# Key and value loads of a decode attention kernel issued from two engines instead of one

## The chip, the cores and the metric

The kernel runs on one core of a Trainium2 chip. The metric is device time in microseconds (us), from launch to end; it ran three times before the change, and a profiled execution of the same kernel gives the trace.

In the profile PE is TensorE (matmuls), PEld its weight loads, DVE is VectorE, ACT is ScalarE, POOL is GpSimd and SP is SyncE. A name with a q at its end (SPq, ACTq, PEq) is the sequencer of that engine, which issues DMAs and waits on semaphores. A DMA queue is shown by a number: q1 is the queue of SP's loads, q10 the queue of ACT's. All queues are worked off by the same 16 DMA engines of the core.

## The reference

One decode step of a transformer block for two tokens (one of each batch row), all in fp32. The attention part reads a cache of keys and values for 32 heads, 8192 positions and 128 channels:

```python
q = (x @ wq)                                    # per head, after a layer norm of x
scores = einsum("bhqd,bhkd->bhqk", q, k_cache) * (Dh ** -0.5)
o = einsum("bhqk,bhkd->bhqd", softmax(scores), v_cache)
h = x + o.reshape(B, 1, H * Dh) @ wo
h2 = h + squared_relu(layernorm(h) @ w1 + b1) @ w2 + b2
```

With B = 2, H = 32 there are 64 pairs (head, batch row), and each pair's keys and values are 2 x 8192 x 128 fp32 values, 8 MB. These 64 loads are 537 of the 561 MB that the kernel reads.

## The kernel before

**The ring.** SBUF holds three slots of 64 KB a partition (`ring[0]` to `ring[2]`, one tensor `slots`). One load, `kvd[i]`, brings all keys and values of pair `i` into slot `i % 3` in one DMA of 128 rows of 64 KB. The projection weights `wq` come first, into slot 2; pairs 0 and 1 go into slots 0 and 1. Every later load goes where an earlier pair has been worked off: load 2 into the slot of `wq`, load `i + 3` into the slot of pair `i`. When pairs 61 and 62 are done, their slots take the weights of the end: `wo` (two DMAs) goes into slot 1, `w1` and `w2` (one DMA and four) into slot 2. The last pair, 63, lies in slot 0.

**Who issues.** SP issues all these loads, each behind a wait for one token of the semaphore FREE (`p.take(sp, FREE)`, which waits for 1 and takes 1 away; line 97 holds the wait). DVE gives one token when the query vectors are ready (line 264) and one behind the last instruction of each pair (line 319). So load 2 takes the first token, load `i + 3` the token of pair `i`, `wo` that of pair 61 and `w1` that of pair 62. Each slot has a semaphore of its own, `LD[t]`, which a load raises by 16 when it has landed.

**A pair.** PE waits for the query column (QUERY) and for the slot's load, and forms the scores of the 8192 positions in two chunks of 4096 (`front`, 16 matmuls a chunk, into one PSUM tile `s[c]` of 128 x 1024 each); it needs the tile back from DVE (BUFFER). DVE takes each chunk's maximum (`maxes`), ACT the exponential with its sum (`exps`), and DVE multiplies the values in the slot by the weights and sums them: four products of 128 x 1024 a chunk (`product`). BUFFER is given behind each chunk's products, FREE behind both chunks. ACT does nothing else in this stage: its loop (line 304) is one pair long, and POOL is idle after it has built the identity at the start (lines 191 to 194).

**The end.** Once pair 62 is done, `shift(0, NG)` brings the pairs 0 to 61 to a common maximum (DVE, one matmul, ACT), then PE forms the scores of pair 63 (lines 405 to 411). The products of pair 63, the combination of all pairs, the projection by `wo`, the second layer norm and the two matmuls of the feed-forward part follow in one chain; PE waits for `w1` at line 467 and for each piece of `w2` at line 491. The result leaves in one small DMA.

Instructions of PE and DVE are recorded first and emitted later, so the profile gives them the one line of that helper, L54; SP's loads all have L159. The pairs' order is set by the program's loops and the semaphores alone; there is no planner.

Of the kernel before, what the change touches and what calls it, by code (L numbers as in the profile page):

```python
# [13 lines left out]
NC = 2  # L14
# [6 lines left out]
LAST = BH - 1  # L21
ROUNDS = LAST // 3
# [77 lines left out]
def attention_block_kernel(nc, xd, kvd, wqd, wod, w1d, w2d, out):  # L100
    p = Program(nc)
    pe, dve, act, pool, sp = p.pe, p.dve, nc.scalar, nc.gpsimd, nc.sync
# [5 lines left out]
    ring = [slots[:, k * ROW : (k + 1) * ROW] for k in range(3)]  # L108
# [42 lines left out]
    LD = [p.sem(f"load{k}") for k in range(3)]  # L151
    SM, LO = p.sem("small"), p.sem("wo_b")
    LW1 = p.sem("w1")
    LW2 = [p.sem(f"w2_{k}") for k in range(len(W2_PIECES))]
    FREE, SCORES, MAXED, EXPED, BUFFER, QUERY = (p.sem(n) for n in ("free", "scores", "maxed", "exped", "buffer", "query"))
    OUT = nc.alloc_semaphore("out")

    def load(tile, src, sem):
        sp.dma_start(tile, src).then_inc(sem, 16)  # L159
# [7 lines left out]
    load(ring[2], wqd, LD[2])  # L167
    load(ring[0], kvd[0], LD[0])
    load(ring[1], kvd[1], LD[1])
    with sp.Fori(0, ROUNDS - 1) as r:  # L170
        i = r * 3
        for u in range(3):
            t = (2 + u) % 3
            p.take(sp, FREE)
            load(ring[t], kvd[i + (2 + u)], LD[t])
    p.take(sp, FREE)
    load(ring[2], kvd[LAST - 1], LD[2])
    p.take(sp, FREE)
    load(ring[0], kvd[LAST], LD[0])
    p.take(sp, FREE)  # L180
    load(WO[:, :HA], wod[:, :HA], LD[1])
    load(WO[:, HA:], wod[:, HA:], LO)
    p.take(sp, FREE)
    load(ring[2][:, :W1_ROW], w1d, LW1)
    at = 0
    for k, n in enumerate(W2_PIECES):
# [5 lines left out]
    p.after("pool", t_id)  # L192
    t_id = p.tell("pool", pool.affine_select(out=ident, in_=ident, compare_op=ALU.not_equal, fill=1.0, base=0,
                                             pattern=[[-1, P]], channel_multiplier=1))
    dve.memset(ones_d, 1.0 / D)
    dve.memset(eps_t, EPS)
    dve.memset(zero, 0.0)
# [69 lines left out]
    def at(tile, pair, n, off=0, size=None):  # L267
        size = n if size is None else size
        return tile[:, bass.ds(pair * n + off, size)]
# [16 lines left out]
    def exps(pair, c):  # L286
        p.take(act, MAXED)
        act.activation(s[c], s[c], AF.Exp, bias=at(nm, pair, NC, c, 1), scale=1.0,  # L288
                       accum_out=at(ls, pair, NC, c, 1)).then_inc(EXPED, 1)
# [6 lines left out]
    first = pe.cut()  # L296
# [4 lines left out]
            front(c, ring[u])  # L301
    pairs = pe.cut()

    with act.Fori(0, ROUNDS * 3) as i:
        for c in range(NC):
            exps(i, c)

# [234 lines left out]
```

## Time and profile before

| | us |
|---|---|
| three runs, median (lowest to highest) | 1302.75 (1302.64 to 1302.89) |
| the profiled execution: its time | 1302.71 |
| its span, from the first to the last instruction | 1301.3 |
| DVE busy | 761.7 (59%) |
| PE busy | 401.4 (31%) |
| ACT busy | 160.3 (12%) |
| POOL busy | 0.7 (0%) |
| DMA: all bytes, mean rate | 561.13 MB, 431 GB/s |

The page gives busy times by engine, shares of the 16 DMA engines by queue, the chain of work that ended last, groups of instructions, and the DMA issues with the time from issue to landing. A timeline gives instructions in order of time; behind a row stands in brackets how long its engine had been idle before it and who ended that. A row that merges several instructions shows their count behind an x, and the stretch from the first to the last. A view by windows gives, for any stretch, the busy time of each engine, the DMA engines' share and rate. Packets are counted in it by their start, so a window of a few us is coarse: one packet of 64 KB counts whole or not at all.

### The profile page before, as it was taken

The numbers are of one execution on the slowest core, as the hardware profiler recorded it, in microseconds if no ns is written. First come the engines' busy times: TensorE is split into PE (matmuls) and PEld (weight loads), VectorE is DVE, ScalarE is ACT, GpSimd is POOL, SyncE is SP. The second block draws the span as 40 slices with busy tenths as digits, with TensorE's granted clock in tenths as the row PEclk, the third lists the DMA queues.
The fourth block names the chain that finished last, engine by engine and source line by source line (L and its number), as shares of the span: only waits on it lengthen the run. The fifth ranks groups of instructions, "written<-read, shape, count | busy, mean of one in ns | idle before, by whom it ended". The sixth has DMA issues, their size and how long they took to land. (4 is left out here: it accounts for less than half of the span.)

```text
span 1301.3 us, 8752 instructions
## 1 busy us (share of the span) xinstructions
PE 401.4 (31%) x2384; PEld 107.9 (8%) x2384; DVE 761.7 (59%) x1267; ACT 160.3 (12%) x268; POOL 0.7 (0%) x6
## 2 busy tenths in 40 slices
PE   3223223323323313313313322322322331331347
PEld 1000000000000000000000000000000000000013
DVE  1375565575565566566466566557457556556564
ACT  0011011011011011111111101101101101101111
POOL 0000000000000000000000000000000000000000
PEclk9576666566666667666666657666666756666668
DMA  9999999999999999999999999999999999999998
GB/s 419 419 449 421 448 421 449 421 437 433 423 445 423 447 423 447 421 443 427 429 439 423 447 423 447 421 447 423 437 433 423 445 423 447 423 447 421 439 423 368
DMA packets 10520, 561.13 MB, mean 431 GB/s; under 512 B 1170, under 2 KB 1298, under 8 KB 1556
## 3 DMA queue, kind: packets, MB, share of 16 engines
q1 hardware_dynamic: 10512, 561.07, 99.7%
q8 instruction: 3, 0.05, 0.0%
q14 instruction: 1, 0.01, 0.0%
q10 hardware_dynamic: 4, 0.00, 0.0%
HBM read 561.00 MB, written 0.07 MB: 431 GB/s over the span
## 5 line engine op out<-in xcount | busy, mean ns | idle before, releaser
L54 PE MATMUL s<-slots,qc 128*32 128x512 f32 x2048 | 362.6, 872 | 859.4 <-PEq L54 859.4
L54 DVE SCALAR_TENSOR_TENSOR slots<-slots,s 128x1024 f32 (+1 forms) x512 | 589.5, 1217 | 2.3 <-DVEq L54 1.0
L54 DVE TENSOR_REDUCE nm<-s 128x1024 f32 (+1 forms) x128 | 156.8, 1225 | 488.9 <-DVEq L54 488.9
L288 ACT ACTIVATE s<-s,nm 128x1024 f32<-128x1024 f32 x128 | 139.3, 1088 | 1090.9 <-ACTq L97 1090.9
L54 PEld LDWEIGHTS s<-slots,qc 128*32 128x32 f32 x2048 | 91.4, 153 | 1129.5 <-issue 1129.4
L54 DVE DVE_READ_ACCUMULATOR slots<-slots,s (+1 forms) x512 | 42.3, 83 | 0.0
L288 ACT ACTIVATION_READ_ACCUMULATOR s<-s,nm (+1 forms) x128 | 24.7, 193 | 0.0
L54 PE MATMUL s<-slots,xr 128*32 128x512 f32 (+1 forms) x96 | 12.6, 684 | 8.8 <-PEq L54 8.2
L54 DVE COPY qc<-qs 128x32 f32 (+1 forms) x64 | 11.0, 172 | 0.0
L54 DVE STREAM_TRANSPOSE big<-s 128x512 f32<-128x512 f32 x2 | 1.4, 718 | 16.1 <-PE s L54 16.1
L54 PE MATMUL pm<-slots,big 128*32 128x512 f32 x64 | 10.6, 782 | 0.0
L54 PE MATMUL pm<-nq,pick_all 128*128 128x496 f32 (+1 forms) x4 | 2.6, 742 | 17.3 <-DVE nq L54 17.3
L54 DVE COPY xT<-pm 128x8 f32<-128x8 f32 x1 | 0.2, 167 | 9.5 <-PE pm L54 9.5
L54 PE MATMUL pm<-ident,xrow 2*128 2x2 f32 x8 | 1.9, 350 | 10.4 <-DMA xrow<-in_x 10.4
L54 PEld LDWEIGHTS s<-slots,xr 128*32 128x32 f32 x96 | 3.5, 126 | 17.1 <-issue 15.7
L54 PE MATMUL s<-big,pick_all 128*128 128x512 f32 x8 | 4.5, 639 | 0.0
L54 PE MATMUL s<-slots,a 128*2 128x128 f32 x112 | 3.5, 272 | 0.9 <-DMA slots<-in_w2d 0.9
L54 PEld LDWEIGHTS pm<-slots,big 128*32 128x32 f32 x64 | 2.6, 138 | 5.6 <-issue 5.1
L54 PEld LDWEIGHTS s<-slots,a 128*2 128x2 f32 x112 | 2.7, 84 | 2.3 <-DVE a L54 1.5
L54 DVE COPY res<-s 128x128 f32<-128x128 f32 x1 | 0.3, 291 | 4.4 <-PE s L54 4.4
L54 PEld LDWEIGHTS pm<-ident,xrow 2*128 2x128 f32 x8 | 1.8, 322 | 10.4 <-DMA xrow<-in_x 10.4
L54 DVE TENSOR_REDUCE gm<-pm 128x62 f32<-128x496 f32 (+1 forms) x2 | 0.9, 426 | 2.9 <-PE pm L54 2.9
(64 smaller groups left out, 29.4 us busy)
## 6 DMA issues: line engine op xcount, KB each, us to landing
slots<-in_wod SPq DMA_DIRECT2D x1, 5120.0 KB, 33.6
slots<-in_w1d SPq DMA_DIRECT2D x1, 3593.0 KB, 31.1
slots<-in_wod SPq DMA_DIRECT2D x1, 3072.0 KB, 40.6
slots<-in_w2d SPq DMA_DIRECT2D x1, 2048.0 KB, 35.6
slots<-in_kvd SPq DMA_DIRECT2D x64, 41.1
slots<-in_w2d SPq DMA_DIRECT2D x1, 1024.0 KB, 37.6
slots<-in_w2d SPq DMA_DIRECT2D x2, 256.0 KB, 37.7
out<-res SPq DMA_DIRECT2D x1, 64.0 KB, 1.6
```

The lines of the kernel that those rows point to most:

```text
L54: ins = getattr(self.engine, op.name)(*op.args, **op.kwargs)
L288: act.activation(s[c], s[c], AF.Exp, bias=at(nm, pair, NC, c, 1), scale=1.0, accum_out=at(ls, pair, NC, c, 1)).then_inc(EXPED, 1)
```

## The change

Three things are written anew.

- SP keeps `wq`, the loads of pairs 0, 1 and 2, every later even pair (4, 6, up to 62), pair 63 and the weights of the end. It takes its tokens from a new semaphore FREE_SP.
- ACT issues the odd pairs 3, 5, up to 61 on its own queue, with tokens of another new semaphore FREE_ACT. For that its loop is unrolled over six pairs (ten rounds; the last three pairs have a small loop). Within each two pairs the load stands behind both exponentials of the even pair: ACT waits there until that even pair is done, then issues the load into its slot.
- POOL, behind the building of the identity, takes each token of FREE and hands it on by turns, the first to SP, then one to ACT and one to SP thirty times, then three to SP.

What DVE and PE do is unchanged, and so is which slot a load fills and which token it stands behind.

```diff
@@ semaphores
-    FREE, SCORES, MAXED, EXPED, BUFFER, QUERY = (p.sem(n) for n in ("free", "scores", "maxed", "exped", "buffer", "query"))
+    FREE, SCORES, MAXED, EXPED, BUFFER, QUERY, FREE_SP, FREE_ACT = (
+        p.sem(n) for n in ("free", "scores", "maxed", "exped", "buffer", "query", "free_sp", "free_act"))
@@ SP's loads
-    with sp.Fori(0, ROUNDS - 1) as r:
-        i = r * 3
+    with sp.Fori(0, (LAST - 3) // 6) as r:
         for u in range(3):
-            t = (2 + u) % 3
-            p.take(sp, FREE)
-            load(ring[t], kvd[i + (2 + u)], LD[t])
-    p.take(sp, FREE)
+            t = (2 + 2 * u) % 3
+            p.take(sp, FREE_SP)
+            load(ring[t], kvd[r * 6 + (2 + 2 * u)], LD[t])
+    p.take(sp, FREE_SP)
     load(ring[2], kvd[LAST - 1], LD[2])
-    p.take(sp, FREE)
+    p.take(sp, FREE_SP)
     load(ring[0], kvd[LAST], LD[0])
-    p.take(sp, FREE)
+    p.take(sp, FREE_SP)
     load(WO[:, :HA], wod[:, :HA], LD[1])
     load(WO[:, HA:], wod[:, HA:], LO)
-    p.take(sp, FREE)
+    p.take(sp, FREE_SP)
     load(ring[2][:, :W1_ROW], w1d, LW1)
@@ POOL, behind the identity
+    def hand_on(to):
+        p.take(pool, FREE)
+        pool.sem_inc(to, 1)
+
+    hand_on(FREE_SP)
+    with pool.Fori(0, (LAST - 3) // 2):
+        hand_on(FREE_ACT)
+        hand_on(FREE_SP)
+    with pool.Fori(0, 3):
+        hand_on(FREE_SP)
@@ ACT's loop
-    with act.Fori(0, ROUNDS * 3) as i:
+    def load_odd(first, t):
+        p.take(act, FREE_ACT)
+        act.dma_start(ring[t], kvd[first + 3]).then_inc(LD[t], 16)
+
+    with act.Fori(0, (LAST - 3) // 6) as r:
+        for u in range(3):
+            for k in range(2):
+                for c in range(NC):
+                    exps(r * 6 + (2 * u + k), c)
+                if k == 0:
+                    load_odd(r * 6 + 2 * u, (2 * u) % 3)
+    with act.Fori(LAST - 3, LAST) as i:
         for c in range(NC):
             exps(i, c)
```

ACT's loop over the pairs, as it stood (ISA is the wait for a maximum; in brackets the semaphore that a row waits for):

```order
L304 UNCONDITIONAL_BRANCH
L288 ISA [waits maxed]
L288 ACTIVATE s,ls<-s,nm 128x1024
L288 ISA [waits maxed]
L288 ACTIVATE s,ls<-s,nm 128x1024
L304 REGISTER_ALU
L304 COMPARE_AND_BRANCH
```

ACT's loop now, the first two of its six pairs:

```order
L319 UNCONDITIONAL_BRANCH
L299 ISA [waits maxed]
L299 ACTIVATE s,ls<-s,nm 128x1024
L299 ISA [waits maxed]
L299 ACTIVATE s,ls<-s,nm 128x1024
L317 ISA [waits free_act]
L317 DMA slots<-in_kvd 128x16384
L299 ISA [waits maxed]
L299 ACTIVATE s,ls<-s,nm 128x1024
L299 ISA [waits maxed]
L299 ACTIVATE s,ls<-s,nm 128x1024
```

Between the second exponential of an even pair and the first of the odd one ACT now waits for the slot's token and issues a load; the other four pairs of a round repeat these rows.

SP's program now, from the last of its loop's three loads to the weights of the end:

```order
L160 ISA [waits free_sp]
L160 DMA slots<-in_kvd 128x16384
L171 REGISTER_ALU
L171 COMPARE_AND_BRANCH
L160 DMA slots<-in_kvd 128x16384 [waits free_sp] x2
L160 DMA slots<-in_wod 128x10240 [waits free_sp]
L160 DMA slots<-in_wod 128x6144
L160 DMA slots<-in_w1d 128x7186 [waits free_sp]
L160 DMA slots<-in_w2d 128x4096
```

The rows read as they did but for the semaphore and the number of rounds, ten in place of twenty; loads 62 and 63 and all weights behind them stay on SP's queue, while load 61, the one ahead of 62, has gone to ACT's.

## The prediction

> **What bounds the kernel now.** I read the page's DMA queues first, then the windows over the pairs, then the chain and the timeline. The queues and the issues:
>
> ```profile
> q1 hardware_dynamic: 10512, 561.07, 99.7%
> slots<-in_kvd SPq DMA_DIRECT2D x64, 41.1
> ```
>
> SP's queue q1 alone keeps the 16 DMA engines busy for 99.7% of the span. The windows ask whether this holds in every stage. Their columns are the stretch and its length, then busy time (and count) of PE, PEld, DVE, ACT and POOL, the granted clock, the DMA engines' share and GB/s:
>
> ```profile
> 62.30:120.40 58.10, 16.51 (x96) 4.21 (x97) 35.08 (x57) 7.22 (x12) 0.00 (x0) 0.65 1.00 433
> 120.40:700.90 580.50, 171.06 (x960) 43.17 (x960) 350.83 (x570) 72.28 (x120) 0.00 (x0) 0.65 1.00 434
> 1165.80:1262.60 96.80, 29.87 (x162) 7.58 (x163) 59.41 (x97) 12.04 (x20) 0.00 (x0) 0.64 1.00 433
> ```
>
> The share is 1.00 and the rate 433 to 434 GB/s at the start, in the middle and at the end of the pairs, while DVE works 350.83 of 580.50 us. So the bytes bound the pairs, with no hole to fill. The timeline shows the beat: PE's first matmul of pairs 60 to 63, the SP issues behind the tokens of pairs 61 and 62, and DVE's rows of pair 62:
>
> ```profile
> 1204.57 5.57 PE L54 MATMUL s<-slots,qc 128*32 128x512 f32 x32 [14.34 <-PEq L54]
> 1223.91 6.13 PE L54 MATMUL s<-slots,qc 128*32 128x512 f32 x32 [13.78 <-PEq L54]
> 1240.89 0.80 SPq L159 DMA_DIRECT2D slots<-in_wod  x2
> 1243.26 5.00 PE L54 MATMUL s<-slots,qc 128*32 128x512 f32 x32 [13.22 <-PEq L54]
> 1246.91 1.22 DVE L54 TENSOR_REDUCE nm<-s 128x1024 f32 x1 [6.15 <-DVEq L54]
> 1248.53 1.23 DVE L54 TENSOR_REDUCE nm<-s 128x1024 f32 x1 [0.40 <-DVEq L54]
> 1259.26 0.33 SPq L159 DMA_DIRECT2D slots<-in_w1d  x1
> 1262.61 3.64 PE L54 MATMUL s<-slots,qc 128*32 128x512 f32 x16 [0.28 <-PEq L54]
> ```
>
> A load lands every 19.35 us (1223.91 to 1243.26). Pair 61 holds its slot for 1240.89 - 1223.91 = 17.0 us, pair 62 for 1259.26 - 1243.26 = 16.0; I take C = 16.5. When a token comes, the next load still lacks 19.35 - 16.5 = 2.85 us and the one after it is whole: 22.2 us of work are queued ahead of the new load, and 22.2 + 19.35 = 41.5 agrees with the 41.1 from issue to landing above. The end hangs on the last bytes:
>
> ```profile
> 1260.11 37.56 DMA slots<-in_w2d
> 1297.72 1.65 PE s L54 x48
> 1299.39 0.29 DVE res L54
> ```
>
> The chain is one DMA wait to 1297.7 and then 2 us of work. Only three things can move the time: the rate of the DMA engines, a hole in their work, or a compute chain of the end that comes later than the last weights.
>
> **The change part by part.** *Issuing.* ACT's issue and POOL's hop are new on the way from a token to a load.
>
> ```profile
> L224 ACTq DMA_DIRECT2D xrow<-in_x x1: 542/542/542, 2.8 to 2.8; - x1
> L159 SPq DMA_DIRECT2D slots<-in_kvd x64: 332/333/426, 1.2 to 1221.0; - x64
> 1.17 0.29 POOL L193 TENSOR_SCALAR_AFFINE_SELECT ident<-ident 128x128 f32<-128x128 f32 x1 [0.23 <-POOL ident L191]
> ```
>
> POOL's only measured wait on a semaphore cost 0.23 us; ACT issues in 0.54 us, SP in 0.33. So a load starts 0.23 to some 0.5 us later than before, and the queued work of many us hides it: 0. Behind ACT's new wait stand the exponentials of the odd pair. They need a maximum that DVE begins after the same token and that takes 1.22 us; ACT needs 0.23 + 0.54 = 0.8. So nothing is late there; without that cover it would be DVE's time, of which 580.50 - 350.83 = 230 of 580 us are idle: 0. The 30 issues that SP loses (30 x 0.33 us) were hidden already: 0. The Trainium skill (DMA: Bandwidth & Descriptors, section Issuing engines are not separate DMA queues) says that all issuers run on the same 16 DMA engines and that issuing from several saves only sequencer time; by it the sum has no term for the rate, and the row of 0.33 us, hidden, agrees.
>
> *Order of service.* Now two queues have loads at once. The trace has one such place: at 2.79 us ACT issues `xrow` (4 KB) on q10, behind three loads of SP. The two issues and PE's first use of `xrow` are from the timeline; the packets and queues are those of the window 2.7 to 10.4 us, from that issue to the landing:
>
> ```profile
> 0.75 0.39 SPq L159 DMA_DIRECT2D slots<-in_wqd  x1
> 2.79 0.54 ACTq L224 DMA_DIRECT2D xrow<-in_x  x1
> DMA packets 52, 3.15 MB, mean 409 GB/s; under 512 B 2, under 2 KB 2, under 8 KB 4
> q1 hardware_dynamic: 48, 3.15, 94.2%
> q10 hardware_dynamic: 4, 0.00, 0.2%
> 10.37 1.86 PE L54 MATMUL pm<-ident,xrow 2*128 2x2 f32 x8 [10.37 <-DMA xrow<-in_x]
> ```
>
> In 7.7 us q1 got 48 packets, three on each engine, and q10 was served in between; SP's three loads would have lasted 58 us. So the queues take turns by packets of about 2.4 us (a load is eight on each engine), and I take equal turns. What that does is worked out by hand. At the token that issues load i+3 let load i+1, ahead of it in its queue, lack r us, and load i+2 in the other queue s us. Both run at half rate, so i+1 lands after 2r. In the C that follow, the other two get C/2 = 8.25 each. At the next token the new s is 19.35 - 8.25 = 11.1 and the new r is s - r - 8.25 = 2.85 - r. So r swings between 0 and 2.85, and at least 11.1 us stay queued in place of 22.2. The engines never run dry, two pairs still take 2 x 16.5 + 2 x 2.85 = 38.7 us, and pairs 0 to 63 cost nothing more: 0.
>
> *The end.* Here the order counts. Load 61 is alone on ACT's queue; 60, 62, 63 and the weights are on SP's. When 62 is issued, 61 lacks 11.1 us and shares the engines until it lands, so 62 has by then got s - r = 8.25 to 11.1 us, in whole packets three or four of 2.4 us: pair 61 starts 7.3 to 11.1 us later than at 1223.91, and I take four packets, 9.7 us, 1233.6. Its token comes at 1233.6 + 16.5 = 1250.1, against 1240.89. Load 62 lands by 1243.26 as before, since all bytes through it have moved by then. So pair 62 follows pair 61 without a wait: its DVE rows take 1259.26 - 1246.91 = 12.35 us, and about 0.5 more, since the second chunk's tile comes back only with pair 61's end and its 16 matmuls then take 1.92 us:
>
> ```profile
> 1266.70 1.92 PE L54 MATMUL s<-slots,qc 128*32 128x512 f32 x16
> ```
>
> The 0.5 is 1.92 - 1.22 (the first maximum) - 0.40 (idle already in the 12.35) = 0.3, and 0.2 for the wait, by POOL's 0.23. That is 12.85. Its token comes at 1262.95, 3.7 us later; with 7.3 and 16.0, or 11.1 and 17.0, it would be 0.8 or 5.6. The DMA queue still holds load 63's rest and `wo` then, and 63 and the weights land when they did. What is late is the combination of the pairs that starts at this token, and with it the chain up to `w1`. That chain has the following slack:
>
> ```profile
> 1290.40 3.21 PE L54 MATMUL s<-slots,xr 128*32 128x448 f32 x32 [0.63 <-DMA slots<-in_w1d]
> 1295.33 1.93 PE L54 MATMUL s<-slots,a 128*2 128x128 f32 x64 [0.66 <-DMA slots<-in_w2d]
> 1297.72 1.60 PE L54 MATMUL s<-slots,a 128*2 128x128 f32 x48 [0.24 <-DMA slots<-in_w2d]
> ```
>
> With the 0.28 us before pair 63's scores (1262.61) PE waits 0.28 + 0.63 + 0.66 + 0.24 = 1.8 us for DMAs; part of the 0.66 is another wait, so I take 1.7. The end moves by 3.7 - 1.7 = +2.0 us, bounds 0 (0.8 is absorbed) and 5.6 - 1.7 = +3.9.
>
> *Sum.* 0 for the pairs, +2.0 at the end. The profiled execution's 1302.71 (0.04 under the median, span 1301.3) gives 1302.71 + 2.0 = **1304.7 us**, 1302.7 to 1306.6 by its own bounds. That is +0.15%. I count a difference up to 0.2%, 2.6 us, as the same: about what a measurement can tell.
>
> **The rivals.** *Order unchanged*: ACT's loads are served whole, as from one queue. Then landings keep their even beat, pair 62 ends on time, and the time is 1302.7. For it: descriptors may be made well ahead of the engines. Against it: `xrow`, served long before SP's queue was empty. The change would then not do what it says.
>
> *Two queues lose at each hand-over* (slower). Place: each packet from load 3 to load 63, 61 x 8 = 488 packets on an engine. It decides from 2.6 us / 488 = 5.3 ns a packet alone, from 1.2 ns together with the +2.0. Bounds: 0, and the 409 GB/s of the `xrow` window against 434, 6% of 61 x 19.35 us = 68 us, though that window counts whole packets (three of 2.4 us in 7.7 us are 94%), so it is nearer 0. I price it at twice the point, 5.2 us: 1302.7 + 2.0 + 5.2 = 1309.9.
>
> *Two queues gain at each hand-over* (faster): the next packet of one queue is prepared while the other's moves. [...] Against it: a share of 1.00 in every window. The windows resolve 1 GB/s of 434, 0.23% or 3 us, so up to 3 us can't be excluded: 1299.7, and if the end is late too, 1301.7. The Trainium skill (DMA: Bandwidth & Descriptors, section Where 436 GB/s comes from) puts the ceiling of the 16 ports at 435.2 GB/s; by it, as an estimate from that page, the rate could rise at most from 433.5 (8.389 MB in 19.35 us) by 0.4%, or about 5 us, to 1298; the 433 to 434 of the windows agree that little is left.
>
> **How the numbers follow.** Equal turns and a late end 0.60, of which 0.42 stay within 0.2% (a shift under 2.6 us lies in the lower two thirds of 0 to 3.9) and 0.18 lie above; order unchanged 0.12, the same; loss at hand-overs 0.14, slower; gain 0.11, faster; 0.03 for what I don't see, split between slower (0.02) and the same (0.01). Faster 0.11, the same 0.55, slower 0.34. The range holds the likeliest case and the unchanged order (0.72), and reaches down to 1300.0 and up to 1308.0 into the two rate cases until some 0.2 are left out.
>
> **What would show it.** In the changed profile the share in the windows stays 1.00 and the rate 433 to 434; a change of 1 GB/s or more there is one of the rate rivals. About half the bytes stand under q10 (30 loads, 252 MB). PE's first matmul of pair 61 comes near 1233.6 in place of 1223.9, and landings come in uneven steps between 16.5 and 22.2 us; an even 19.35 with pair 61 at 1223.9 means unchanged order. The `w1` issue moves from 1259.26 to about 1263, load 63's first matmul goes with it, and PE's waits for `w1` and `w2` shrink or vanish. The prediction is wrong if a window in the pairs falls under 1.00, or if ACT's wait for a maximum gives way to DVE waiting on ACT.

## The result

The changed kernel takes 1306.53 us (median of 8 runs, 1305.46 to 1308.54) against 1302.78 (8 runs, 1302.55 to 1302.89): a ratio of 1.003, 95% interval 1.0019 to 1.0041. It is slower, by about 3.8 us. The runs of the kernel before lie within 0.4 us, those of the changed one within 3.1.

The profiled execution is one of the fastest of the changed kernel, 1305.48 us with a span of 1303.9; a second profile of the same kernel (called *again* below) has 1307.57 and 1306.2. The queues of the changed kernel:

```profile
q1 hardware_dynamic: 6192, 309.41, 54.9%
q10 hardware_dynamic: 4324, 251.66, 44.6%
```

ACT's queue carries 30 loads, 252 MB, and the two together keep the engines as busy as one did (99.5% against 99.7%). Whether the rate suffers is seen from the bytes that have moved by a given time. The next rows are the windows 0 to 117, 0 to 300 and 0 to 1200 us, first of the kernel before:

```profile
DMA packets 852, 50.28 MB, mean 430 GB/s; under 512 B 82, under 2 KB 82, under 8 KB 84
DMA packets 2220, 129.40 MB, mean 431 GB/s; under 512 B 242, under 2 KB 242, under 8 KB 244
DMA packets 8914, 519.86 MB, mean 433 GB/s; under 512 B 978, under 2 KB 978, under 8 KB 980
```

and of the changed kernel:

```profile
DMA packets 852, 50.23 MB, mean 429 GB/s; under 512 B 82, under 2 KB 82, under 8 KB 84
DMA packets 2196, 128.82 MB, mean 429 GB/s; under 512 B 226, under 2 KB 226, under 8 KB 228
DMA packets 8902, 519.02 MB, mean 433 GB/s; under 512 B 978, under 2 KB 978, under 8 KB 980
```

At 433.5 MB a millisecond the changed kernel is 0.1 us behind at 117 us, 1.3 behind at 300 and 1.9 at 1200 (0.84 MB). These windows count packets by their start, so each is good to some 0.5 us. The trace's records of single packets say it more finely: between 118.7 and 120 us up to 14 of the 16 engines stand idle, nowhere else are more than one or two; the lag is 0.3 us before that and 1.9 to 2.1 from 250 us on, and it doesn't grow any more. So there is one hole, near 119 us, and no loss of rate in the thousand microseconds after it. The engines' idle time makes about half of it: the 16 engines lose 0.9 us of their time from 118 to 122 us. The rest lies in the first packets of the next load: ACT issues load 5 at 118.67, its packets start from 119.64 on, 1.0 us later, and each engine's first one takes 2.7 to 3.6 us in place of 2.42. The windows from 262 to 1262 us, the kernel before and the changed one, have the same rate:

```profile
262.00:1262.00 1000.00, 290.59 (x1634) 73.53 (x1634) 607.46 (x988) 124.96 (x208) 0.00 (x0) 0.65 1.00 433
262.00:1262.00 1000.00, 293.36 (x1664) 73.75 (x1664) 608.15 (x989) 125.36 (x208) 0.00 (x0) 0.65 1.00 433
```

The other part is the end. The changed kernel's first matmuls of pairs 61 and 62 and its later steps, from the timelines of PE and SP:

```profile
1234.62 6.08 PE L54 MATMUL s<-slots,qc 128*32 128x512 f32 x32 [13.83 <-PEq L54]
1246.99 3.30 PE L54 MATMUL s<-slots,qc 128*32 128x512 f32 x16 [6.29 <-PEq L54]
1251.56 1.92 PE L54 MATMUL s<-slots,qc 128*32 128x512 f32 x16 [1.26 <-PEq L54]
1251.68 0.80 SPq L160 DMA_DIRECT2D slots<-in_wod  x2
1264.75 0.33 SPq L160 DMA_DIRECT2D slots<-in_w1d  x1
1293.86 3.21 PE L54 MATMUL s<-slots,xr 128*32 128x448 f32 x32
1298.51 1.93 PE L54 MATMUL s<-slots,a 128*2 128x128 f32 x64 [0.38 <-DVE a L54]
```

Pair 61 starts 10.7 us later than before (1234.62 against 1223.91), the token of pair 62, which `w1` follows, comes 5.5 us later (1264.75 against 1259.26), and PE no longer waits for any weight: the bracket before `w1`'s matmuls is gone, and the one before `w2`'s names DVE. So the chain that ended last, which was one DMA wait before, now runs through the compute of the end (four of its 31 pieces; dots stand for the others):

```profile
1273.74 0.16 DVE slots L54
...
1278.70 7.34 PE pm L54 x42
...
1292.97 4.15 PE s L54 x34
...
1298.51 3.50 PE s L54 x120
```

### The profile page after: what moved, and what is told of

Its sections match the earlier page's. It is cut to its first block, busy times and chain, and to the rows that moved or that the text cites. A ratio compares the mean times of both kernels' runs of the same rounds, so it can differ in the third digit from the quotient of the medians.

```text
span 1303.9 us, 8771 instructions
## 1 busy us (share of the span) xinstructions
PE 403.5 (31%) x2384; PEld 107.2 (8%) x2384; DVE 761.4 (58%) x1267; ACT 160.4 (12%) x268; POOL 0.7 (0%) x6
## 5 line engine op out<-in xcount | busy, mean ns | idle before, releaser
L54 DVE TENSOR_REDUCE nm<-s 128x1024 f32 (+1 forms) x128 | 156.7, 1224 | 492.8 <-DVEq L54 492.8
L54 PEld LDWEIGHTS s<-slots,xr 128*32 128x32 f32 x96 | 3.5, 126 | 16.5 <-issue 16.5
```

The source lines that it names most:

```text
L54: ins = getattr(self.engine, op.name)(*op.args, **op.kwargs)
```

## The experiments

**Theory**: two queues take turns by packets. Where sharing begins, two loads land together and the next one stands in the queues alone, so the engines that finish it first may run dry: a hole, once. At the end load 61, alone on ACT's queue, is late by half a load, and the chain behind pair 62 with it. **Rivals**: each hand-over between the queues costs (3.8 us for 30 loads, 0.13 us a load); issuing through POOL and ACT costs; a second queue's first load has a fixed cost.

### One load on ACT's queue, in the middle

Based on the changed kernel; SP issues all loads but 33, and POOL hands 31 tokens to SP, one to ACT, 32 to SP.

```diff
-    with act.Fori(0, (LAST - 3) // 6) as r:
...
+    with act.Fori(0, 30) as i:
+        for c in range(NC):
+            exps(i, c)
+    for c in range(NC):
+        exps(30, c)
+    load_odd(30, 30 % 3)
+    with act.Fori(31, LAST) as i:
+        for c in range(NC):
+            exps(i, c)
```

> One load alone, 33, goes to ACT's queue; all others stay on SP's. Theory (a hole where sharing begins, and a late end): 32 and 33 land together, so for the 17 us of pair 32 only load 34 is queued, and the engines that finish it first stand idle, once, for about 1.4 us, near 700 us, as at 119 us in the changed kernel. Later the order is that of one queue and the end is on time behind the last byte: 1302.7 + 1.4 to 1.9 = 1304.1 to 1304.6. Rival (each hand-over between the queues costs): the changed kernel's +3.8 us for 30 loads is 0.13 us a load, so 1302.8 to 1302.9. Rival (issuing through POOL and ACT costs, by token): POOL hands on all 64 tokens here too, so 1305 to 1306.5.

Measured: 1304.80 us (11 runs, 1303.15 to 1305.63), a ratio of 1.0015 (1.0006 to 1.0023). One load of 64 on the second queue costs 1.9 us against its own series of the kernel before (1302.93), half of what 30 cost and 15 times the 0.13 us a load of the hand-over rival. The profile of this run was its fastest, so the kernel was run once more for another:

> Load 33 alone on ACT's queue once more, for a second profile: the first was the fastest of its eleven runs (1303.15 of up to 1305.63) and had almost no hole. Theory: a run near 1304.8 has its token of pair 32 later against the end of load 34, and bytes late by 1.5 to 2 us from 700 us on.

That run took 1304.63. Its matmuls of the pairs 31 to 33 (PE), then ACT's issue of load 33 and SP's of load 35:

```profile
643.67 5.56 PE L54 MATMUL s<-slots,qc 128*32 128x512 f32 x32 [14.36 <-PEq L54]
682.37 4.99 PE L54 MATMUL s<-slots,qc 128*32 128x512 f32 x32 [33.13 <-PEq L54]
693.80 3.64 PE L54 MATMUL s<-slots,qc 128*32 128x512 f32 x16 [6.45 <-PEq L54]
640.38 0.37 ACTq L323 DMA_DIRECT2D slots<-in_kvd  x1
698.65 0.34 SPq L160 DMA_DIRECT2D slots<-in_kvd  x1
```

and the bytes moved by 690 and by 1200 us:

```profile
DMA packets 5124, 298.74 MB, mean 433 GB/s; under 512 B 562, under 2 KB 562, under 8 KB 564
DMA packets 8902, 519.08 MB, mean 433 GB/s; under 512 B 978, under 2 KB 978, under 8 KB 980
```

Load 32 is a whole load late (682.37 - 643.67 = 38.7 us), pair 33 follows directly, and load 35 is issued at 698.65, when load 34 has been alone for some 16 us (by the events of its semaphore, load 33 had all landed at 682.9). The first of the 16 engines ended load 34 at 699.4, by the events of its semaphore. At 690 us the bytes are those of the kernel before to the packet; at 1200 they are 0.78 MB, 1.8 us, behind. The end is on time behind the bytes again. The hole is where the theory puts it; the expected 1304.1 to 1304.6 was just missed. In the fastest run load 32 came earlier by one packet's turn (first matmul at 679.85), load 35 was issued at 696.91, 2.6 us ahead of the first engine's end, and the bytes were 0.6 us behind at 1200 (by the single packets 0.3, against 1.5 in the other run).

### One load on ACT's queue, near the end

```diff
-    with act.Fori(0, (LAST - 3) // 6) as r:
...
+    with act.Fori(0, 58) as i:
+        for c in range(NC):
+            exps(i, c)
+    for c in range(NC):
+        exps(58, c)
+    load_odd(58, 58 % 3)
+    with act.Fori(59, LAST) as i:
+        for c in range(NC):
+            exps(i, c)
```

> One load alone, 61, goes to ACT's queue. Theory: 60 and 61 land together near 1224, pair 60 starts there in place of 1204.6, its token comes near 1241, 61 and 62 follow without a wait, 13 us each, so w1 is issued near 1267.3 in place of 1259.3; a hole of about 1.4 us falls at 1241. The chain from there to the end took 37.3 us in the changed kernel, so the end comes at 1304.6 in the span and the time is 1307.5 to 1308.5: more than with 30 loads on ACT's queue. Rival (each hand-over costs, 0.13 us a load): 1302.9. Rival (issuing through POOL costs): 1305 to 1306.5.

Measured: 1309.52 us (6 runs, 1305.62 to 1310.74), 1.0047 (1.0035 to 1.0059). The timeline of its profile (1309.11):

```profile
1224.00 5.02 PE L54 MATMUL s<-slots,qc 128*32 128x512 f32 x32 [33.11 <-PEq L54]
1235.46 3.64 PE L54 MATMUL s<-slots,qc 128*32 128x512 f32 x16 [6.45 <-PEq L54]
1249.96 3.64 PE L54 MATMUL s<-slots,qc 128*32 128x512 f32 x16 [6.28 <-PEq L54]
1240.15 0.33 SPq L160 DMA_DIRECT2D slots<-in_kvd  x1
1267.72 0.33 SPq L160 DMA_DIRECT2D slots<-in_w1d  x1
```

Pair 60 at 1224.0, its token at 1240.2, `w1` at 1267.7: as worked out (1224, 1241, 1267.3). The median came 1 us above the range; in the profile `w1` is 0.4 us later than worked out, and the chain from there took 41.4 us with what lies around the span, against 40.7 in the first profile of the changed kernel. The hole at 1241 is there too, somewhat smaller than expected: down to 6 of the 16 engines are busy, and 0.9 us are lost by the single packets. One load costs 6.6 us here, more than the 30 loads of the change, which neither a price by load nor one by hand-over can give.

### The last odd loads back on SP's queue

The changed kernel with 57, 59 and 61 on SP; POOL's alternation and ACT's six-pair loop end six pairs earlier.

```diff
-    with sp.Fori(0, (LAST - 3) // 6) as r:
+    with sp.Fori(0, 9) as r:
...
+    for i in range(56, LAST - 1):
+        p.take(sp, FREE_SP)
+        load(ring[i % 3], kvd[i], LD[i % 3])
```

> As the changed kernel, but the last three odd loads, 57, 59 and 61, stay on SP's queue. Theory: the hole at 119 us stays (bytes late by 1.9 us from there on), but the pairs of the end catch up, w1 is issued about 1.9 us later than before the change and no more, and the time is 1302.7 + 1.9 = 1304.6 (1304.2 to 1305.0), with less spread from run to run than the changed kernel's 1305.5 to 1308.5. Rival (each hand-over costs): 27 of 30 loads, 1306.1.

Measured: 1304.56 us (11 runs, 1303.32 to 1305.70), 1.0012 (1.0004 to 1.0021), at the expected 1304.6; the spread is 2.4 us against 3.1, little less. In its profile (1304.98) PE's waits for the weights are back, and the chain that ended last is again one DMA wait:

```profile
1262.01 0.33 SPq L160 DMA_DIRECT2D slots<-in_w1d  x1
1292.49 3.21 PE L54 MATMUL s<-slots,xr 128*32 128x448 f32 x32 [0.86 <-DMA slots<-in_w1d]
1297.42 1.93 PE L54 MATMUL s<-slots,a 128*2 128x128 f32 x64 [0.66 <-DMA slots<-in_w2d]
1299.80 1.61 PE L54 MATMUL s<-slots,a 128*2 128x128 f32 x48 [0.24 <-DMA slots<-in_w2d]
```

The piece of that chain, and the bytes moved by 1200 us:

```profile
1262.87 36.89 DMA slots<-in_w2d
DMA packets 8901, 518.95 MB, mean 432 GB/s; under 512 B 978, under 2 KB 978, under 8 KB 980
```

The bytes are 0.91 MB behind (518.95 against 519.86), 2.1 us, and the time is 2.3 above the kernel before's profile. So without the late end only the hole is left, and all of it is in the time.

### ACT's queue from load 33 on

```diff
+    with act.Fori(0, 30) as i:
+        for c in range(NC):
+            exps(i, c)
-    with act.Fori(0, (LAST - 3) // 6) as r:
+    with act.Fori(5, 10) as r:
```

> ACT issues only the odd loads 33 to 61, the first half stays on one queue. Theory: the hole of 1.4 to 1.9 us moves from 119 us to about 700 us, the end is as late as in the changed kernel, and the time is that of the changed kernel, 1305.5 to 1307, median near 1306.3. Rival (each hand-over costs): half the loads, 1304.6. Rival (the hole belongs to the start, by code loading or the like): no hole, 1304.5.

Measured: 1305.54 us (11 runs, 1303.96 to 1306.47), 1.0019 (1.0010 to 1.0028). This is at the lower edge of the expected range and above the rivals' 1304.5 and 1304.6, but by only 1 us in a spread of 2.5; the time alone would not tell them apart. The profile does, and it misses a part of the expectation. There is no hole at all, though one of 1.4 to 1.9 us was expected near 700 us (519.81 MB by 1200 us, 0.05 behind), and its 1306.24 comes from the end alone:

```profile
1233.83 5.52 PE L54 MATMUL s<-slots,qc 128*32 128x512 f32 x32 [14.40 <-PEq L54]
1250.21 3.64 PE L54 MATMUL s<-slots,qc 128*32 128x512 f32 x16 [0.93 <-PEq L54]
1264.83 0.33 SPq L160 DMA_DIRECT2D slots<-in_w1d  x1
1294.84 3.21 PE L54 MATMUL s<-slots,xr 128*32 128x448 f32 x32
```

ACT's issue of load 35, and the bytes moved by 1200 us:

```profile
697.05 0.34 ACTq L323 DMA_DIRECT2D slots<-in_kvd  x1
DMA packets 8914, 519.81 MB, mean 433 GB/s; under 512 B 978, under 2 KB 978, under 8 KB 980
```

No hole was also the sign of the rival that ties the hole to the start of the kernel. But load 33 alone had one at 699 us, so that rival is out. The issue of load 35 (697.05) says why there is none here: it comes 2.4 us ahead of the first engine's end of load 34 (699.49 by its semaphore), as in the fastest run of load 33 alone, where 2.6 us left almost no hole. A fixed cost of the second queue's first load would have shown here as well.

With the bytes on time, pair 61 is 9.9 us late (1233.83 against 1223.91) and `w1` 5.6. Together with the run before, where the bytes were late and the end was not, this separates the two parts of the cost.

### Issuing alone

First, all loads on SP, with POOL handing on each token; then all loads from 3 on, and the weights, on ACT's queue.

```diff
-    with pool.Fori(0, (LAST - 3) // 2):
-        hand_on(FREE_ACT)
-        hand_on(FREE_SP)
-    with pool.Fori(0, 3):
+    with pool.Fori(0, 64):
         hand_on(FREE_SP)
```

> All loads stay on SP's queue, but POOL hands every token on to SP. Theory (only the sharing of two queues costs): the later issue is hidden by 22 us of queued work, 1302.8, within 0.3 us of the kernel before. Rival (issuing through POOL costs, by token): 1305 to 1306.5.

```diff
+    with act.Fori(0, 20) as r:
+        for u in range(3):
+            for c in range(NC):
+                exps(r * 3 + u, c)
+            load_odd(r * 3 + u, u)
```

> ACT issues every load from 3 on, with the weights of the end, on its own queue; SP issues only wq and the loads 0 to 2. Theory: one queue at a time serves the loads in order, but there is one crossing at the start, where load 3 on ACT's queue shares with load 2: 2 and 3 land together near 102 us, then load 4 comes behind 3 on one queue; whether a hole opens at 119 us as in the changed kernel is the same question of one lone load, so up to 2 us there, nothing at the end: 1302.8 to 1304.8. Rival (ACT's issue or POOL's hop costs by load): twice the 30 loads' +3.8 us, 1310. Rival (hand-overs cost): 1302.9.

Measured: 1302.74 us with POOL's hop (11 runs, 1302.60 to 1303.12), 0.9999 (0.9990 to 1.0008): it costs nothing. With all on ACT 1304.20 (11 runs, 1303.39 to 1305.90), 1.0012 (1.0003 to 1.0021): with twice the issues of the change, less than half its loss, and the bytes of its profile are 0.85 MB, 2.0 us, behind by 1200 us (1.5 us by the single packets), with a hole again near 119 us. The profiled time, 1305.57, is 2.9 us longer than the kernel before's, more than the bytes say, because the hole does not make the 16 engines late alike: the last of them ends load 5 3.1 us later than before (142.60 against 139.48) and load 63 2.8 us later (1265.11 against 1262.32). What is left there is the one crossing from SP's queue to ACT's.

### A longer hold, to size the cover

Three DVE instructions that do nothing for the result, then seven, ahead of each pair's token, in the kernel before and in the one with load 33 alone.

```diff
             ins.then_inc(BUFFER, 1)
+        for extra, n in ((big, 8), (aw, 4), (acc, 4)):
+            row = pick_all[:, None, :].to_broadcast([P, n, P])
+            dve.tensor_tensor(extra.rearrange("p (a m) -> p a m", m=P), row, row, op=ALU.mult)
         dve.drain().then_inc(FREE, 1)
```

> The kernel before, with three idle DVE instructions (128 x 1024, 512 and 512) ahead of each pair's token, about 1.25 + 0.67 + 0.67 = 2.6 us a pair. Theory: a pair holds its slot 19.1 instead of 16.5 us, and the 22 us of queued work hide it in all pairs; the token of pair 62 comes 2.6 us later, of which the end's slack takes 1.7 or more: 1302.8 to 1303.7.

> The same three idle DVE instructions in the kernel with load 33 alone on ACT's queue. Theory: at the one place where load 34 is queued alone, there is no cover, so the later token lengthens the hole one to one: that kernel's +1.9 us grows to about 4.5 us over the kernel before with the same instructions, 1307 to 1308. Rival (each hand-over costs): the difference stays 0.1 us. Rival (a fixed cost of a second queue's first load): the difference stays 1.9 us.

> The kernel before with seven idle DVE instructions ahead of each pair's token, about 5.3 us a pair (with the three earlier ones of 2.4 us the token of pair 62 came 2.1 us later and the end absorbed all of it). Theory: the queued work still hides it in all pairs; the token of pair 62 comes about 5 us later, of which the end absorbs about 2.9: 1304.9 (1304 to 1306).

> The same seven instructions with load 33 alone on ACT's queue. Theory (no cover where load 34 is queued alone): a hole opens when the token of pair 32 comes less than about 2 us ahead of the first engine's end of load 34; in the two profiles so far it came 2.6 us ahead (bytes late by 0.25 us) and 0.9 us ahead (late by 1.25). Now it comes about 2 us behind, so the bytes are late by about 4 us from there on, and the time is that of the kernel before with the same instructions plus 3 to 5: 1309 (1308 to 1310). Rival (a fixed cost of the second queue's load): plus 1.9, 1306.8. Rival (each hand-over): plus 0.1, 1305.0.

| | kernel before | load 33 on ACT's queue |
|---|---|---|
| as it is | 1302.85 (33 runs) | 1304.80 (11 runs) |
| three more instructions | 1302.96 (11 runs), 1.0001 (0.9992 to 1.0010) | 1304.40 (11 runs), 1.0016 (1.0006 to 1.0025) |
| seven more instructions | 1305.87 (9 runs), 1.0024 (1.0014 to 1.0034) | 1306.15 (9 runs), 1.0028 (1.0018 to 1.0038) |

Each ratio is taken against the kernel before as it ran in the same series; its medians there were 1302.85 to 1302.93.

The kernel before behaved as expected: the queued work hides a longer hold, and what is lost with seven instructions is lost at the end. The other column refutes the one-to-one growth: both expectations were about 3 us too high. With seven instructions the two kernels differ by 0.3 us, so that by time alone this pair doesn't exclude the rival with a cost by hand-over; with three they differ by 1.4. The timeline of the kernel with seven instructions shows why the hold doesn't come through: ACT's issue of load 33, the first matmul of pair 32, SP's issue of load 35, and `w1`'s:

```profile
645.49 0.37 ACTq L323 DMA_DIRECT2D slots<-in_kvd  x1
677.14 5.64 PE L54 MATMUL s<-slots,qc 128*32 128x512 f32 x32 [28.36 <-PEq L54]
699.20 0.34 SPq L160 DMA_DIRECT2D slots<-in_kvd  x1
1266.25 0.33 SPq L160 DMA_DIRECT2D slots<-in_w1d  x1
```

Load 33 is issued 5.1 us later than without the instructions (640.38), so load 32 has the engines to itself for longer and lands 5.2 us earlier (677.14 against 682.37). The token of pair 32 is 0.55 us later, not 5.3. The hole followed the token: the bytes are 518.88 MB by 1200 us, 2.3 us behind, against 1.8. And the chain of the end, late already from its seven instructions (`w1` at 1265.56 in that form of the kernel before), hides most of it. So the theory of the hole stands on where it is and when it opens, not on this size; my mistake was to take the landing of load 32 as fixed.

### The changed kernel once more

> The changed kernel once more, for a second profile: its runs lie between 1305.5 and 1308.5. Theory: in a run slower than 1305.5 the bytes are again late only by a hole near 119 us (0 to 2 us), their rate is unchanged afterwards, and w1 is issued later than in the first profile (1264.8); the time is set by that issue plus about 40 us. Rival (the rate of two queues varies): the lag of the bytes grows over the pairs.

Measured: 1307.42 us (5 runs, 1306.34 to 1308.06), 1.0032 (1.0018 to 1.0045). The bytes are 1.0 us behind by 300 us (128.95 MB) and 1.9 by 1200 in windows, 1.2 us at both by the single packets: a hole near 119 us again, and a lag that doesn't grow over the pairs. `w1` is issued at 1266.55, 1.8 us later than in the first profile, and the time is 2.1 us longer. Of the 1.8, 0.4 stand at the token of pair 61 already (1252.05 against 1251.68); 1.4 come in pair 62, in its second chunk. The next rows are windows over the two chunks of pair 62 (the third column from the end is the granted clock; the DMA share and GB/s stand behind it); the changed kernel's first profile, then the second:

```profile
1246.90:1250.40 3.50, 3.30 (x16) 0.68 (x16) 3.50 (x7) 0.00 (x0) 0.00 (x0) 0.58 1.12 487
1251.50:1253.50 2.00, 1.92 (x16) 0.50 (x16) 1.23 (x1) 0.00 (x0) 0.00 (x0) 1.00 1.21 524
```

```profile
1247.30:1251.00 3.70, 3.63 (x16) 0.68 (x16) 3.70 (x7) 0.00 (x0) 0.00 (x0) 0.50 0.78 337
1251.90:1255.60 3.70, 3.64 (x16) 0.68 (x16) 1.23 (x1) 1.21 (x2) 0.00 (x0) 0.50 0.86 372
```

The same 16 matmuls take 1.92 us at a granted clock of 1.00 and 3.64 at 0.50, and DVE stands idle for the difference ahead of the second maximum (0.26 us in the first profile, 1.98 in the second). The Trainium skill (TensorE: Matmul & The Clock Gate, section Part 1: The HAM clock gate (the "warmup" mystery)) says that the clock follows a free-running window of activity of about 3.4 us, and that the number of slow matmuls therefore differs from run to run for one kernel. These two profiles agree that it differs; they don't test the window.

## Why the prediction was right, and where not

Time and sign. The forecast was 1304.7 with a range of 1300.0 to 1308.0; 1306.5 lies in the range, but on the side that had 0.34, not in the likeliest class: it is +0.29%, not +0.15%. The likeliest case, equal turns and a late end, is what happened, in the part of it (0.18 of 0.60) that lay above 0.2%; its size was too small by 1.8 us, in two terms of the sum. That the time lies just under the sum's own upper bound, 1306.6, is in part luck: that bound has no term for the hole.

- **Bound by bytes, rate unchanged by two queues**: right. 433 GB/s from 262 to 1262 us in both kernels, and a lag that doesn't grow over a thousand microseconds; neither rate rival took place. The sign named for them, 1 GB/s in a window, was too fine: the prediction's own stretches read 432, 435 and 431 GB/s from 120.4 us on, against 434, 433 and 433, up and down by whole packets counted at their start.
- **Issuing through POOL and ACT at 0**: right, 1302.74 with POOL's hop. ACT's issue was not tried without a crossing, but with 61 loads on it the lag by single packets stays at 1.5 us from 140 us to the end.
- **Turns by packets**: right. Pair 61 was to start 9.7 us late; it was 9.9 in the run with no hole before it, four packets of 2.4 us. The single packets show the turns themselves: from 600 to 645 us each engine takes one of SP's and one of ACT's in alternation wherever both have work. The unchanged order is refuted by it.
- **Uneven steps of 16.5 to 22.2 us**: only at first. In the first profile PE's first matmuls of the pairs 5 to 12 come 14.5 to 26.8 us apart, but from 286 us on every 19.35 us, as before the change, each pair late by about half a load (pair 60 at 1215.28 in place of 1204.57). The working allows that as well: at r = 2.85/2 = 1.43 the swing stops. An even beat was therefore no sign of unchanged order by itself.
- **"The engines never run dry"**: wrong, and the first mis-sized term, 0 against 1 to 2 us. The step worked out the steady turn, in which at least 11.1 us stay queued, and let it begin at once. The crossing from one queue's order to two was left out. There i+2 and i+3 run at half rate together, land together, and for the 16 to 17 us of pair i+2 load i+4 is alone with its 19.35: 2 to 3 us of cover instead of 11, of which the first engine, which ends 1.5 to 2.1 us ahead of the last, has the least.
- **Pair 62 in 12.85 us**: too small, by 0.2 us in one profile and by 1.6 in two, the second mis-sized term. From token to token it took 13.1, 14.5 and 14.5 (first profile, *again*, ACT from 33 on). The 1.92 us for the second chunk was taken from a row at full clock; at half clock it is 3.64.
- **Slack of 1.7 us at the end**: somewhat too small. With three more DVE instructions `w1` came at 1261.35, 2.1 us late, and the end absorbed it all (1302.97 in the profile); with `w1` 5.5 to 7.3 us late the times were 2.8 to 4.9 us longer than 1302.71. So the slack is 2.0 to 2.7 us.
- **The sum of the end**: +2.0 forecast; measured +2.8 (first profile) and +4.9 (*again*), and +3.5 where no hole was in it. The hole and the end don't simply add: the later bytes shift pair 61 too, but also give the chain more room at `w1`.

The hole's size follows one quantity in all ten profiles that have a crossing: how far ahead of the first engine's end of the lone load the next load is issued. By the growth of the lag in the single packets, 2.6 and 2.4 us ahead lost 0.2 and 0.1 us, 1.1 ahead 0.9, 0.9 ahead 1.0 to 1.2 (three profiles), 0.7 ahead 1.5, 0.4 ahead 1.7, and 0.3 ahead 1.9 and 2.3.

Not settled: why this lead differs between runs of one kernel. With load 33 alone, what differs is whether load 32 lands a packet's turn earlier (first matmul at 679.85 or 682.37); which queue gets the first turn on each engine, and why, these runs don't show.

No version beat the kernel before. With one queue at a time at the end, 1304.56, the hole remains; the best of the changed forms is the one in which nothing is shared, 1302.74, and that is the kernel before with a hop.

## What to carry to other kernels

Where one queue already keeps the DMA engines busy, as here (99.7%, 433 GB/s with one queue and with two), don't expect rate from a second one; it changes the order of landing: the load that is needed first shares the engines with one that is needed later, and comes half a load late. Work out the crossing as well as the steady state, from what stands queued when the next token comes; and look at the last loads, where lateness can't be made up. One load on a second queue can cost more than thirty, if it is the one ahead of the end.

## What was unexpected of the hardware

- A load must be issued well ahead of the end of the work that the engines still have. Its packets started 1.0 us after the issue (119.64 after 118.67, 699.61 after 698.65), and an engine's first one took up to 3.6 us in place of 2.42: issued 0.7 us ahead of the first engine's end, load 35 of the kernel with load 33 on ACT's queue cost 1.5 us, issued 2.6 us ahead 0.2.
- The same matmuls at the same place of the same program, 1.92 us in one run and 3.64 in another, made 1.4 us of the 2.1 between two runs of the changed kernel. The kernel before repeats within 0.4 us in its first series and within 0.9 over all; that its waits for the weights take up such differences is likely but wasn't tried.
